# Early keys, values and q loaded with four rows to a partition, pooled keys out transposed, q turned by products with the identity

## The chip, the cores and the metric

The kernel runs on one core of one Trainium2 chip. The metric is the device time of one execution in microseconds (us), as the median of several runs. Lower is better.

## What is computed

Three stages in a row, all in float32: attention of every token over keys and values that are averaged in groups of 8 rows, an expert with a squared ReLU, and a gated expert.

```python
batch, n_heads, seq, head_dim = (8, 8, 576, 64)
k_p = k.reshape(B, H, Sp, pool, D).mean(axis=3)        # pool = 8, Sp = 72
v_p = v.reshape(B, H, Sp, pool, D).mean(axis=3)
scores = scale * np.matmul(q, k_p.transpose(0, 1, 3, 2))
attn = np.exp(scores - np.max(scores, axis=-1, keepdims=True))
attn = attn / (np.sum(attn, axis=-1, keepdims=True) + 1e-09)
x = np.matmul(attn, v_p)                               # then (B * S, H * D) = (4608, 512)
x = np.maximum(x @ w_in, 0.0) ** 2 @ w_out             # d_ff = 2048
out = (1.0 / (1.0 + np.exp(-(x @ w_gate))) * (x @ w_val)) @ w_out2   # d_ff = 1536
```

The weights of both experts arrive as 64-bit floats and are rounded to 32 bits on the chip.

## The kernel before

The 4608 tokens are worked in nine blocks of 512. The first expert runs block by block in passes over its 16 column tiles f: for each f four groups of three products make h (line 798), ScalarE and VectorE square it and split it into a high and a low part (lines 841 to 854), and twelve products with the output weights add to four banks (line 807). A float32 product is made of three products of such high and low parts. The first pass takes block 0 and only the tiles f = 0 to 7, the second takes block 1 and all 16.

Each weight tile has to be converted before its first use: a load of 512 KB (`raw_w`), a 64-bit add on GpSimd (line 235), one step on ScalarE (line 241), four on VectorE (lines 245 to 256), a copy of the high part on ScalarE (line 272) and a subtraction on VectorE (line 276). 32 such conversions (`in` 0 to 15, `out` 0 to 15) run during the first two passes.

Ahead of the first pass stands the attention of block 0, and within it that of block 1. Their keys, values and q come in by `early_kv` and `early_q`, which this change touches; the attention of later blocks is prepared in another way (`prep`, `load_q`) and is untouched. Before, an early k or v is loaded as three tiles with two rows of each head to a partition. Pooling is then a product with the constant `pm` as the stationary operand, 72 columns wide, and 512 columns of data moving (`pool_rows`, line 641). Pooled keys are copied to SBUF (line 674), turned by four transposes (line 679) and placed in `kpT` by two copies (line 683). q is loaded as it lies, one row to a partition, and is turned by 16 transposes of 128x128 (line 722). After that come scores (line 456), softmax in pieces on VectorE and ScalarE (lines 478 to 511), a turn of the weights (line 534), a copy (line 542), and the product with v (line 553).

The order of all instructions on each engine is written out beforehand by a planner (`Plan.run`). It simulates the engines with given durations (`op("pe", 0.88, ...)`), ranks and buffers, and each engine then runs its list strictly in that order. Loads and stores all stand in the list of SyncE (SP). The loaded tiles of early k, v and q lie in slots of the weight tiles; `convert_w1(n)` puts its raw tile in the slot of weight n + 4, so it waits until a load that was there has been used up. The numbers `n1 - 8` and so on in the calls choose these slots.

Of the kernel before, what the change touches and what calls it, by code (L numbers as in the profile page):

```python
# [131 lines left out]
def kernel(  # L132
# [12 lines left out]
    nc = tc.nc  # L145
# [197 lines left out]
    pm = att.tile([128, 160], F32, name="pm")  # L343
# [284 lines left out]
    rows = [(0, 128), (128, 128), (256, S // 2 - 256)]  # L628

    def load2(src, be, j, get):  # L630
        t = get()
        r0, rn = rows[j]
        nc.sync.dma_start(
            out=t[0:rn], in_=src[be, :, 2 * r0:2 * (r0 + rn), :].rearrange("h (p r) d -> p h (r d)", r=2))
        return t

    def pool_rows(src, st, j, r, bank):
        if j == 0 and r == 0:
            st["p"] = ps(*bank)
        r0, rn = rows[j]  # L640
        nc.tensor.matmul(
            out=st["p"][0:SP, :], lhsT=pm[0:rn, 64 - r0 // 4:64 - r0 // 4 + SP], rhs=src[j][0:rn, :, r],
            start=(j == 0 and r == 0), stop=(j == 2 and r == 1))

    def early_kv(be, src, n, rank, bank, consts, is_k):
        tiles, st = {}, {}
        prev, lds = [], []
        hold = be > 0
        for j in range(3):
            def ld(j=j):  # L650
                tiles[j] = load2(src, be, j, lambda: wpool.tile(
                    [128, H, 2, D], F32, tag=w1_tag(n + j), name="rows2"))

            lds.append(op("dma", (2.0, 2.0, 0.6)[j], ld, rank=rank + 0.1 * j, take=(w1_tag(n + j),), lag=2.0))
        for j in range(3):
            for r in range(2):
                o = op("pe", 0.88, lambda j=j, r=r: pool_rows(tiles, st, j, r, bank),
                       (lds if hold else lds[j:j + 1]) + prev + consts, rank + 4,
                       take=(bank[0],) if j == 0 and r == 0 else (), give=(w1_tag(n + j),) if r else ())
                prev = [o]  # L660
# [4 lines left out]

        if not is_k:
            o = op("act", 0.5, evac_v, prev, rank + 6, give=(bank[0],))
            for h in range(H):
                v_ready[be, h] = o
            return  # L670

        def evac_k():
            st["kp"] = kp = att.tile([SP, DM], F32, tag="kv", name="kp0", bufs=3)
            nc.scalar.activation(out=kp, in_=st["p"][0:SP, :], func=ACTF.Copy)

        def tr():
            st["p"] = p = ps(*bank)
# [10 lines left out]
        o = op("act", 0.5, evac_k, prev, rank + 5, take=("kv",), give=(bank[0],))  # L688
        o = op("pe", 0.3, tr, [o], rank + 6, take=(bank[0],), give=("kv",))
        o = op("act", 0.3, lambda: place(0), [o], rank + 7)  # L690
        o = op("act", 0.3, lambda: place(1), [o], rank + 7, give=(bank[0],))
# [3 lines left out]
    def early_q(b, rank, later, gets, takes, out_of, out_take, banks, consts):  # L695
        tiles = {}
        loads = []
        for hf in range(2):
            for j in range(NTA):
                def ld(j=j, hf=hf):  # L700
                    if j % 2 == 0 and hf == 0:
                        tiles["s"] = gets[j // 2]()
                    if hf == 0:
                        tiles[j] = tiles["s"][:, j % 2]
# [702 lines left out]
```

## Time and profile before

| What | Value |
|---|---|
| median of 3 runs | 1755.55 us (1755.24 to 1757.31) |
| profiled execution, its own time | 1755.72 us |
| its span | 1753.9 us |
| TensorE (PE) busy | 1732.8 us, 99% |
| VectorE (DVE) busy | 1103.3 us, 63% |
| ScalarE (ACT) busy | 799.3 us, 46% |
| GpSimd (POOL) busy | 239.5 us, 14% |
| mean granted TensorE clock | 0.993 of full speed |

The time is the span and 1.8 us around it. Busy means that an engine has an instruction under way. The shares are means over the whole execution: the change concerns its first 70 us or so, and has to be read from there.

### The profile page before, as it was taken

What the parts mean: (1) busy time and instruction counts of PE and PEld (TensorE: products, weight loads), DVE (VectorE), ACT (ScalarE), POOL (GpSimd) and SP (SyncE); (2) the same over time, 40 slices, a digit from 0 to 9 for tenths busy, and PEclk for the clock granted to TensorE, in tenths of its full rate; (3) what the DMA queues carried; (4) which work ended last, traced back from release to release, by engine and by line L of the source; (5) the groups of instructions that cost most, each with busy time, mean ns of one, the idle gap of its engine ahead of it and who ended that gap; (6) DMA issues with size and microseconds to landing.
All of it is one profiled execution on the core that took longest, in us unless ns stands there. A gap on an engine that the chain in (4) does not pass through costs nothing.

```text
span 1753.9 us, 24006 instructions
## 1 busy us (share of the span) xinstructions
PE 1732.8 (99%) x8624; PEld 1491.5 (85%) x8624; DVE 1103.3 (63%) x2066; ACT 799.3 (46%) x1946; POOL 239.5 (14%) x186
## 2 busy tenths in 40 slices
PE   7999999999999999999999999999999999999999
PEld 4678877878888888878888999999999999999998
DVE  7999758888686765523465555555555665655554
ACT  5676654453444343322345444445444444444442
POOL 1600000010001000000131112122111212111100
PEclk9999999999999999999999999999999999999999
DMA  9732244554544333020111222223333333333321
GB/s 259 267 88 74 53 104 106 148 155 121 142 106 128 99 95 105 31 86 1 60 49 61 72 73 85 73 97 120 109 109 109 120 120 120 109 109 109 108 73 49
DMA packets 183063, 179.71 MB, mean 102 GB/s; under 512 B 79008, under 2 KB 124832, under 8 KB 182944
## 3 DMA queue, kind: packets, MB, share of 16 engines
q1 hardware_dynamic: 182944, 178.18, 34.1%
q8 instruction: 68, 1.11, 0.3%
q14 instruction: 51, 0.42, 0.1%
HBM read 120.59 MB, written 49.28 MB: 97 GB/s over the span
## 4 chain that ended last, share of the span: by engine, by line
PE 93%; DMA 0%; DVE 0%; ACT 0%; issue 0%; ACTq 0%
PE acc L807 21%; PE h L798 21%; PE h L1190 17%; PE acc L1305 17%; PE att L1190 9%; PE acc L1190 4%; PE att L553 2%; PE att L456 2%; DMA y_dram<-y 0%; PE att L399 0%; ACT x L789 0%; DVE kp L390 0%; DVE e L511 0%; DVE g L854 0%; DVE o L1331 0%
## 5 line engine op out<-in xcount | busy, mean ns | idle before, releaser
L807 PE MATMUL acc<-g,out 128*128 128x512 f32 x1728 | 422.0, 393 | 0.0
L798 PE MATMUL h<-x,in 128*128 128x512 f32 x1728 | 421.0, 392 | 0.0
L807 PEld LDWEIGHTS acc<-g,out 128*128 128x128 f32 x1728 | 320.9, 188 | 72.7 <-issue 4.7
L798 PEld LDWEIGHTS h<-x,in 128*128 128x128 f32 x1728 | 321.3, 188 | 69.7 <-issue 2.0
L841 ACT ACTIVATE r<-h 128x512 f32<-128x512 f32 x144 | 86.0, 597 | 281.7 <-PE h L798 269.7
L1305 PE MATMUL acc<-in,p 128*128 128x512 f32 x648 | 182.6, 390 | 0.0
L1305 PE MATMUL acc<-out,p 128*128 128x512 f32 x648 | 182.2, 389 | 0.0
L847 DVE TENSOR_TENSOR r<-r,h 128x512 f32<-128x512 f32 x112 | 76.5, 684 | 133.7 <-ACT r L841 133.5
L1212 ACT ACTIVATE res<-h 128x384 f32<-128x384 f32 x144 | 70.7, 492 | 193.3 <-PE h L1190 187.0
L1305 PEld LDWEIGHTS acc<-out,p 128*128 128x128 f32 x648 | 121.6, 188 | 25.8
L1305 PEld LDWEIGHTS acc<-in,p 128*128 128x128 f32 x648 | 121.3, 188 | 23.9
L854 DVE TENSOR_TENSOR g<-r,g 128x512 fp32r<-128x512 f32 x144 | 103.4, 718 | 47.8 <-ACT g L851 46.4
L235 POOL INT64_ADD raw<-raw x40 | 43.7, 1093 | 592.1 <-DMA raw<-in_moe_w_out_dram 285.9
L851 ACT ACTIVATE g<-r 128x512 fp32r<-128x512 f32 x144 | 91.1, 633 | 67.9 <-DVE r L847 63.2
L1221 DVE TENSOR_TENSOR res<-res,acc 128x384 f32<-128x384 f32 x72 | 39.6, 551 | 120.4 <-PE acc L1190 116.8
L1331 DVE TENSOR_TENSOR o<-o,acc 128x512 f32<-128x512 f32 x72 | 49.4, 688 | 93.9 <-PE acc L1305 93.8
L1190 PE MATMUL h<-in,in 128*128 128x384 f32 x432 | 99.8, 339 | 3.8 <-ACT res L1212 3.8
L486 ACT ACTIVATE e<-att,m 128x72 f32<-128x72 f32 x272 | 82.9, 320 | 38.3 <-DVE m L478 38.2
L1190 PE MATMUL h<-out,in 128*128 128x384 f32 x432 | 99.7, 338 | 0.0
L1023 POOL TENSOR_TENSOR yt<-yf 128x768 f32<-128x768 f32 x32 | 59.8, 1870 | 291.9 <-DMA yf<-y_dram 257.4
L1271 ACT ACTIVATE p<-res 128x384 fp32r<-128x384 f32 x144 | 73.7, 523 | 55.7 <-DVE res L1265 55.5
L1190 PE MATMUL h<-in,out 128*128 128x384 f32 x432 | 98.0, 334 | 0.0
(140 smaller groups left out, 2707.0 us busy)
## 6 DMA issues: line engine op xcount, KB each, us to landing
yf<-y_dram SPq DMA_DIRECT2D x16, 1536.0 KB
o_part<-o SPq DMA_DIRECT2D x72, 256.0 KB
o<-o_part SPq DMA_DIRECT2D x72, 256.0 KB
y_dram<-y SPq DMA_DIRECT2D x36, 256.0 KB
w_dram<-t SPq DMA_DIRECT2D x36, 256.0 KB
w2s<-w_dram SPq DMA_DIRECT2D x36, 256.0 KB
out_dram<-o SPq DMA_DIRECT2D x36, 256.0 KB
raw_w<-in_moe_w_in_dram SPq DMA_DIRECT2D x15, 512.0 KB
```

The costliest lines, as they stand in the source:

```text
L486: nc.scalar.activation(out=e[:, h, 0:SP], in_=p[:, h * SP:(h + 1) * SP], func=ACTF.Exp, bias=m[:, h:h + 1], accum_out=z[:, h:h + 1])
L798: nc.tensor.matmul(out=h[:, 0:n], lhsT=w[:, a, kk * 128:(kk + 1) * 128], rhs=xs[kk][:, c], start=(kk == 0 and i == 0), stop=(kk == KT - 1 ...
L807: nc.tensor.matmul(out=y_ps[m][:, 0:NA], lhsT=w[:, a, m * 128:(m + 1) * 128], rhs=g_t[f][:, c], start=(f == f0 and i == 0), stop=(f == f1 ...
L841: nc.scalar.activation(out=r, in_=st["h"][:, 0:NA], func=ACTF.Relu)
L847: nc.vector.tensor_tensor(out=st["r"], in0=st["r"], in1=st["h"][:, 0:NA], op=ALU.mult)
L851: nc.scalar.activation(out=g[:, 0], in_=st["r"], func=ACTF.Copy)
L854: nc.vector.tensor_tensor(out=g_t[f][:, 1], in0=st["r"], in1=g_t[f][:, 0].bitcast(F32), op=ALU.subtract)
L1023: nc.gpsimd.tensor_tensor(out=t, in0=q(a), in1=q(c), op=ALU.subtract)
L1190: nc.tensor.matmul(out=st[which, z][:, 0:HN], lhsT=w[:, wa, col:col + 128], rhs=ys[y, k2][:, yc], start=(first[z] == m and k2 == 0 and j = ...
L1212: nc.scalar.activation(out=new((which, key)), in_=st[which, z][:, 0:HN], func=ACTF.Copy)
L1271: nc.scalar.activation(out=p_t[fi][:, 0, h * HN:(h + 1) * HN], in_=st["gate", key], func=ACTF.Copy)
L1305: nc.tensor.matmul(out=o_ps[i], lhsT=p_t[f][:, a, i * 128:(i + 1) * 128], rhs=wslot[c, "out", f][:, w], start=(f == 0 and j == 0), stop=(f ...
```

## The change

Early k and v are now loaded as four tiles, two for each half of the heads, with four rows of each head to a partition: 128 partitions (64 pooled rows' worth) and 16 partitions (8 pooled rows' worth). `pm` is 64 columns wide and sums two partitions. For k the data is now the stationary operand, 64 columns (one head) at a time, and `pm` moves with 64 or 8 columns; heads 2i and 2i + 1 go to the lower and the upper 64 partitions of the result, which is thus already turned. The copy to SBUF and the four transposes fall away. For v `pm` stays stationary, with 64 and 8 columns, and 256 columns of data move. q comes as one tile for each half of the heads with four rows to a partition, and is turned by full products with the identity, 64 columns stationary and 128 moving, which write every fourth column. The planner gets new durations, and the loads take other slots.

```diff
-        nc.vector.memset(pm, 0.0)
-            out=pm[:, 64:96], in_=ident.rearrange("p (n r) -> p n r", r=POOL // 2), op=ALU.add, axis=AX.X)
+            out=pm, in_=ident.rearrange("p (n r) -> p n r", r=POOL // 4), op=ALU.add, axis=AX.X)
-    rows = [(0, 128), (128, 128), (256, S // 2 - 256)]
-    def pool_rows(src, st, j, r, bank):
-        nc.tensor.matmul(
-            out=st["p"][0:SP, :], lhsT=pm[0:rn, 64 - r0 // 4:64 - r0 // 4 + SP], rhs=src[j][0:rn, :, r],
-            start=(j == 0 and r == 0), stop=(j == 2 and r == 1))
+    R = 4
+    rows = [(0, 128), (128, S // R - 128)]
+    def pool_values(src, st, bank):
+        for hf in range(2):
+            for r in range(R):
+                n0 = 0
+                for j, (_, rn) in enumerate(rows):
+                    n = rn * R // POOL
+                    nc.tensor.matmul(
+                        out=st["p"][n0:n0 + n, 256 * hf:256 * hf + 256], lhsT=pm[0:rn, 0:n],
+                        rhs=src[hf, j][0:rn, :, r], start=(r == 0), stop=(r == R - 1), skip_group_check=True)
+                    n0 += n
+    def pool_keys_t(src, st, hf, bank):
+        for pr in range(2):
+            n0 = (2 * hf + pr) * SP
+            for j, (_, rn) in enumerate(rows):
+                n = rn * R // POOL
+                for r in range(R):
+                    for i in range(2):
+                        nc.tensor.matmul(
+                            out=st["p"][64 * i:64 * i + 64, n0:n0 + n], lhsT=src[hf, j][0:rn, 2 * pr + i, r],
+                            rhs=pm[0:rn, 0:n], start=(r == 0), stop=(r == R - 1), skip_group_check=True)
+                n0 += n
...
-        def evac_k():
-        def tr():
-            for pr in range(KT):
-                nc.tensor.transpose(
-                    p[:, pr * SP:(pr + 1) * SP], st["kp"][:, pr * 128:(pr + 1) * 128], ident[0:SP, 0:SP])
...
-                for j in range(NTA):
-                    nc.tensor.transpose(
-                        p[:, 128 * j:128 * (j + 1)], tiles[j][:, 2 * pr:2 * pr + 2].rearrange("p h d -> p (h d)"), ident)
+                for r in range(R):
+                    for i in range(2):
+                        nc.tensor.matmul(
+                            out=p[64 * i:64 * i + 64, r:NA:R], lhsT=tiles[hf][:, 2 * (pr % 2) + i, r], rhs=ident,
+                            start=True, stop=True)
...
-    early_kv(0, k, n1 - 8, -0.5, ("acc3", 1), [c2], True)
+    early_kv(0, k, n1 - 20, -0.5, ("acc3", 1), [c2], True)
-    early_kv(0, v, n1 - 14, V0L, ("acc3", 1), [c2], False)
+    early_kv(0, v, n1 - 16, V0L, ("acc3", 1), [c2], False)
-    early_kv(1, k, n1 - 17, t1 - P1, K1B, [c2], True)
+    early_kv(1, k, n1 - 12, t1 - P1, K1B, [c2], True)
-    early_kv(1, v, n1 - 11, t1 - P1 + V1L, K1B, [c2], False)
+    early_kv(1, v, n1 - 8, t1 - P1 + V1L, K1B, [c2], False)
```

The planner's order moves with it. In the rows below the tile names carry a number for the buffer; `rows` are the loaded tiles, `kp` pooled keys, `att`, `h` and `acc` PSUM banks.

First place: TensorE's list from its start to the first scores. Before (key pooling, turns of pooled keys, first half of q, scores):

```order
L641 MATMUL acc_102<-rows_95,pm 72x512 x2
L641 MATMUL acc_102<-rows_98,pm 72x512 x2
L641 MATMUL acc_102<-rows_100,pm 72x512 x2
L679 MATMUL acc_126<-ident,kp_122 128x72 x4
L722 MATMUL acc_146<-ident,rows_112 128x128 x2
L722 MATMUL acc_146<-ident,rows_119 128x128 x2
L456 MATMUL att<-kpT_78,qT_158 128x144 x2
L456 MATMUL h<-kpT_78,qT_158 128x144 x2
```

After, of the same place:

```order
L654 MATMUL acc_105<-pm,rows_94 64x64 x8
L654 MATMUL acc_105<-pm,rows_97 64x8 x8
L726 MATMUL acc_189<-ident,rows_q 64x128 x8
L726 MATMUL acc_200<-ident,rows_q 64x128 x8
L726 MATMUL acc_218<-ident,rows_q 64x128 x8
L726 MATMUL acc_230<-ident,rows_q 64x128 x8
L455 MATMUL att<-kpT_78,qT_209 128x144 x2
L455 MATMUL h<-kpT_78,qT_209 128x144 x2
```

All of q's turns now stand ahead of the first scores, where only the first half of them stood.

Second place: ScalarE's list from the first exponentials on (`e` softmax weights, `vp` pooled values, `aT` turned weights). Before:

```order
L486 ACTIVATE e,z<-att,m 128x72 x4
L499 ACTIVATE e<-e 128x4x72
L486 ACTIVATE e,z<-att,m 128x72 x4
L499 ACTIVATE e<-e 128x4x72
L664 ACTIVATE vp<-acc_193 72x512
L726 ACTIVATE qT_250<-acc_238 128x512
```

After:

```order
L485 ACTIVATE e,z<-att,m 128x72 x4
L498 ACTIVATE e<-e 128x4x72
L485 ACTIVATE e,z<-att,m 128x72 x4
L677 ACTIVATE vp<-acc_276 72x512
L541 ACTIVATE aT<-acc_319 72x16x32
L541 ACTIVATE aT<-acc_333 72x16x32
L498 ACTIVATE e<-e 128x4x72
```

The fourth exponential of the first half now stands behind the copy of pooled values and behind two copies of turned weights.

Third place: TensorE's list at the end of the first pass, where the last turns of block 1's attention weights stand (line 534 before, 533 after). Before:

```order
L798 MATMUL h<-x,in_142 128x512 x6
L399 MATMUL att<-ident,kp 128x72
L534 MATMUL att<-ident,e_80 72x128 x4
L399 MATMUL att<-ident,kp 128x72
L534 MATMUL att<-ident,e_81 72x128 x4
L807 MATMUL acc_612<-g,out_1114 128x512 x3
L807 MATMUL acc_618<-g,out_1114 128x512 x3
```

After:

```order
L803 MATMUL h<-x,in_216 128x512 x6
L812 MATMUL acc_767<-g,out_1189 128x512 x3
L812 MATMUL acc_777<-g,out_1189 128x512 x3
L812 MATMUL acc_788<-g,out_1189 128x512 x3
L812 MATMUL acc_795<-g,out_1189 128x512 x3
L398 MATMUL att<-ident,kp 128x72
L533 MATMUL att<-ident,e_80 72x128 x4
L533 MATMUL att<-ident,e_81 72x128 x4
```

The last twelve products of the pass now stand ahead of the two turns, and stood behind them.

## Rows read from the trace of the kernel before

**Rows 1.** The page, its first lines: busy us (share of span) xinstructions.

```profile
span 1753.9 us, 24006 instructions
...
PE 1732.8 (99%) x8624; PEld 1491.5 (85%) x8624; DVE 1103.3 (63%) x2066; ACT 799.3 (46%) x1946; POOL 239.5 (14%) x186
```

**Rows 2.** Windows by stage: busy us of each engine, TensorE's clock, DMA share, GB/s.

```profile
16.00:35.00 19.00, 18.06 (x78) 11.02 (x79) 16.59 (x38) 13.34 (x50) 4.29 (x4) 0.85 1.17 291
35.00:54.70 19.70, 19.14 (x52) 6.37 (x50) 19.43 (x31) 10.81 (x20) 11.09 (x9) 0.74 0.97 319
54.70:77.00 22.30, 19.86 (x105) 15.86 (x105) 21.09 (x28) 17.79 (x43) 16.46 (x13) 1.00 0.97 331
77.00:111.00 34.00, 34.00 (x186) 27.02 (x185) 29.44 (x63) 26.12 (x78) 1.15 (x1) 1.00 0.08 20
111.00:115.00 4.00, 2.02 (x15) 1.49 (x14) 3.86 (x12) 2.63 (x12) 0.00 (x0) 1.00 0.36 69
115.00:930.00 815.00, 815.00 (x3887) 662.26 (x3886) 547.50 (x1042) 359.24 (x970) 65.13 (x60) 1.00 0.35 94
```

**Rows 3.** Waits of TensorE over the span: us in total, times, longest.

```profile
PE acc L641 <- DMA rows<-in_k_dram: 5.0, 1, 5.0
PE att L534 <- DVE e L511: 4.4, 4, 1.3
PE att L456 <- ACT qT L726: 2.1, 1, 2.1
```

**Rows 4.** Timeline of TensorE, 0 to 55 us: start, us, what [idle before].

```profile
5.01 6.95 PE L641 MATMUL acc<-rows,pm 128*72 128x512 f32 x12 [5.01 <-DMA rows<-in_k_dram]
12.74 0.44 PE L679 MATMUL acc<-ident,kp 72*128 72x72 f32 x4 [0.78 <-ACT kp L674]
13.02 1.04 PE L722 MATMUL acc<-ident,rows 128*128 128x128 f32 x8
...
31.48 1.08 PE L553 MATMUL acc<-aT,vp 72*64 72x512 f32 x4
32.49 0.76 PE L456 MATMUL h<-kpT,qT 128*128 128x144 f32 x4
...
34.19 2.79 PE L641 MATMUL att<-rows,pm 128*72 128x512 f32 x6
36.82 1.47 PE L534 MATMUL acc<-ident,e 128*72 128x128 f32 x12
...
54.66 1.66 PE L798 MATMUL h<-x,in 128*128 128x512 f32 x6
```

**Rows 5.** Timeline of TensorE, a product with v in block 1.

```profile
91.80 1.10 PE L553 MATMUL att<-aT,vp 72*64 72x64 f32 x12
92.83 3.02 PE L798 MATMUL h<-x,in 128*128 128x512 f32 x12
```

**Rows 6.** Timeline of SyncE's queue, the early loads of q and what follows.

```profile
4.33 6.63 SPq L708 DMA_DIRECT2D rows<-in_q_dram  x6
...
29.91 7.87 SPq L708 DMA_DIRECT2D rows<-in_q_dram  x10
37.82 0.50 SPq L231 DMA_DIRECT2D raw_w<-in_moe_w_out_dram  x1
```

**Rows 7.** Windows of 2 us, columns as in rows 2.

```profile
18.00:20.00 2.00, 2.00 (x11) 2.00 (x10) 1.92 (x5) 1.77 (x10) 0.00 (x0) 0.50 1.14 243
...
46.00:48.00 2.00, 2.00 (x7) 0.38 (x4) 2.00 (x3) 1.25 (x3) 2.00 (x2) 0.50 1.05 391
```

**Rows 8.** Groups of VectorE: line 251 in 42.5 to 77.3, then 77.3 to 124.

```profile
L251 DVE SCALAR_TENSOR_TENSOR t_w<-raw_w,t_w 128x512 uint32<-128x512 uint32 x5 | 6.4, 1283 | 0.2
...
L251 DVE SCALAR_TENSOR_TENSOR t_w<-raw_w,t_w 128x512 uint32<-128x512 uint32 x9 | 6.2, 684 | 0.0
```

**Rows 9.** Timeline of GpSimd's adds, and of VectorE at TensorE's second wait.

```profile
45.96 10.11 POOL L235 INT64_ADD raw_w<-raw_w  x7 [0.32 <-DMA raw_w<-in_moe_w_out_dram]
...
73.73 0.96 DVE L511 TENSOR_TENSOR e<-e,z 128x288 f32<-128x288 f32 x1
```

More of the change, by code (lines that the diff above doesn't have):

```diff
@@ L645, in early_kv @@
     def early_kv(be, src, n, rank, bank, consts, is_k):
         tiles, st = {}, {}
[L647 to L660, printed above, removed]
+        lds = []
@@ new lines, in early_kv, with ld @@
+        for hf in range(2):
+            for j, (r0, rn) in enumerate(rows):
+                x = 2 * hf + j
+                def ld(hf=hf, j=j, r0=r0, rn=rn, x=x):
+                    tiles[hf, j] = t = wpool.tile([128, 4, R, D], F32, tag=w1_tag(n + x), name="rows4")
+                    nc.sync.dma_start(
+                        out=t[0:rn],
+                        in_=src[be, 4 * hf:4 * hf + 4, R * r0:R * (r0 + rn), :].rearrange("h (p r) d -> p h (r d)", r=R))
+                lds.append(op("dma", (1.65, 0.3)[j], ld, rank=rank + 0.1 * x, take=(w1_tag(n + x),), lag=2.0,
+                              after=lds[-1:]))
@@ L664, in evac_v @@
             nc.scalar.activation(out=vp_t[be].rearrange("n h d -> n (h d)"), in_=st["p"][0:SP, :], func=ACTF.Copy)
+        tags = tuple(w1_tag(n + x) for x in range(4))
         if not is_k:
-            o = op("act", 0.5, evac_v, prev, rank + 6, give=(bank[0],))
+            o = op("pe", 3.5, lambda: pool_values(tiles, st, bank), lds + consts, rank + 4, take=(bank[0],), give=tags)
+            o = op("act", 0.6, evac_v, [o], rank + 6, give=(bank[0],))
             for h in range(H):
@@ L686, in place @@
                 scale=kscale)
[L688 to L691, printed above, removed]
+        prev = []
+        for hf in range(2):
+            o = op("pe", 1.8, lambda hf=hf: pool_keys_t(tiles, st, hf, bank),
+                   (lds if be else lds[2 * hf:2 * hf + 2]) + prev + consts,
+                   rank + 4, take=(bank[0],) if hf == 0 else (), give=tags[2 * hf:2 * hf + 2])
+            prev = [o]
+        o = op("act", 0.4, lambda: place(0), [o], rank + 7)
+        o = op("act", 0.4, lambda: place(1), [o], rank + 7, give=(bank[0],))
         for pr in range(KT):
@@ L698, in early_q, with ld @@
         for hf in range(2):
[L699 to L713 removed]
+            def ld(hf=hf):
+                tiles[hf] = t = gets[hf]()
+                for off, m, be, s0 in parts(b):
+                    nc.sync.dma_start(
+                        out=t[off // R:(off + m) // R],
+                        in_=q[be, 4 * hf:4 * hf + 4, s0:s0 + m, :].rearrange("h (p r) d -> p h (r d)", r=R))
+            loads.append(op("dma", 1.65, ld, rank=rank + later * hf, take=(takes[hf],), lag=2.0, after=loads[-1:]))
         res = []
@@ L727, in ev @@
                     out=out_of(pr).rearrange("p a g t -> p (a g t)"), in_=st["p"], func=ACTF.Copy)
[L729 to L731 removed]
+            o = op("pe", 0.9, tr, [loads[hf]] + consts, rank + 5 + pr, take=(bank[0],),
+                   give=(takes[hf],) if pr % 2 else ())
+            res.append(op("act", 0.6, ev, [o], rank + 6 + pr, take=(out_take(pr),) if out_take(pr) else (),
                           give=(bank[0],)))
```

33 lines of the change are left out of this document (7 added, 26 removed).

## The prediction

> **What bounds the kernel now.** I start with the page. TensorE is busy for 1732.8 of 1753.9 us [rows 1], so only 21 us are there to be won by waiting less, and the rest by giving TensorE less to do. The windows by stage say where: from 115 to 930 us TensorE never pauses [rows 2]. An early gain is therefore kept in full, and an early loss is paid in full: what counts is when TensorE gets to the end of the first pass, at about 115 us. The list of its waits gives 5.0 us for the first keys, 2.1 us for turned q and 4.4 us in four pieces for softmax weights from VectorE [rows 3]. There is no wait for any other early load in it.
>
> Next I put TensorE and VectorE side by side, stage by stage [rows 2]. From 16 to 35 us TensorE is idle for 0.94 us and VectorE for 2.41; from 35 to 54.7 us it is 0.56 and 0.27; from 54.7 to 77 us 2.44 and 1.21. So after 16 us two engines are full at once. VectorE's work there is softmax and the conversion of weights, and this change takes none of it away. It is also slow there: one step of a conversion (line 251) takes 1283 ns up to 77 us and 684 ns behind that [rows 8], and the difference goes with GpSimd, which adds without pause from 46 to 56 us [rows 9] and for 16.46 us of the window to 77 [rows 2]. From 77 to 111 us TensorE alone is full. From 111 to 115 us it waits again for VectorE, 1.98 us. So there are two places where TensorE is tied to VectorE: about 73 to 75 us, where VectorE's last step before the second turn starts at 73.73 [rows 9], and 111 to 115 us. A gain on TensorE ahead of 73 us is only worth what VectorE brings along.
>
> **The change part by part.** All prices of TensorE are for its higher clock (2.4 GHz) first.
>
> Pooling before: three products take 2.63 us, from 34.19 to 36.82 [rows 4], 0.877 us each. There are 24 (two keys, two values, six each): 21.0 us. Turning pooled keys: 0.44 us [rows 4] twice, 0.9. Turning q: 8 transposes in 1.04 us [rows 4], 16 for each block: 4.2 us for both. Sum 26.1 us.
>
> After, everything but the scores is 64 columns wide, with two results in different halves of the partitions. The trace has such products in line 553: 64 wide, in pairs. One pair with 512 columns takes 1.01 us, from 31.48 to 32.49 [rows 4], where two products of that length one after another would take 1.75. So a pair does lie side by side. In block 1 two pairs with 64 columns and one with 384 take 1.03 us, from 91.80 to 92.83 [rows 5]; the long one is 0.75 x 1.01 = 0.76, which leaves 0.135 us for a short pair.
> - One k: 16 pairs with 64 columns moving and 16 with 8. At 0.135 us each 4.3 us. No row shows 8 columns moving; from below they cost 8/512 of 1.01 us, 0.016, and the 64-column pairs 0.126, together 2.3 us. I take 4.3, since the short pair is the nearest row and is itself dearer than its columns.
> - One v: eight times 256 columns for 64 rows, with the 8-row product in the upper half beside it: 8 x 0.505 = 4.0 us. If these two don't lie side by side it is 16 x 0.44 = 7.0 us.
> - One q: 16 pairs with 128 columns, 0.25 us each, 4.0 us; singly 7.0.
>
> After in all 2 x (4.3 + 4.0 + 4.0) = 24.6 us, so TensorE's work shrinks by 1.5 us, with bounds of 5.5 us less (k at 2.3) and, with nothing side by side (k then 8.6), 19 us more. The gain in work is small: the products are shorter but there are many more.
>
> Here a rule speaks against the change. The Trainium skill, TensorEngine Tiling (Array Packing), section Key Properties, says that a change of tiling mode drains TensorE, and v's products change between 128 partitions by 64 columns and 16 partitions by 8 at every step. By the rule v would be nearer to 7.0 than to 4.0. No row here changes mode at every product, so this stays among the rivals.
>
> ScalarE loses two copies of pooled keys. It is not full in any of these stages [rows 2], so I set them at nothing. VectorE loses one clear and sums twice as many columns of the constant, both ahead of 5.0 us, where everything waits for keys: nothing.
>
> Loads: the same bytes. For q six issues took 6.63 us of SP's queue, and ten took 7.87 us [rows 6]; now it is two and four. The first raw tile behind all early loads is issued at 37.82 [rows 6]; it will go out several microseconds sooner. What it triggers is that GpSimd's adds start sooner, and so does VectorE's slow phase, partly over softmax. I price this at nothing: as many adds fall on as much work, only earlier.
>
> Order: all of q's turns stand ahead of the first scores, an extra 2.0 us at the high clock. They have to wait for the second half of q, but ScalarE's copies hold the scores back anyway (2.1 us before [rows 3]). If that cover is gone, first scores come 1 to 2 us later. On ScalarE the fourth exponential now stands behind the copy of pooled v and two copies of turned weights. Queued behind it are the exponentials of the second half, and VectorE waits for these. Both go against the gain.
>
> The likeliest sum. VectorE's idle time from 16 to 77 us is 2.41 + 0.27 + 1.21 = 3.9 us, and it is idle because TensorE and ScalarE are late with scores and exponentials. With pooling of v shorter I let it win back three quarters: -2.9 us, with bounds from +3 (the two new waits above) to -3.9. At the second tie the last twelve products of the pass, 3.0 us of work [rows 5], now stand ahead of the two turns and fill the 1.98 us [rows 2]; but they wait for VectorE's last conversion, so I count two thirds: -1.3 us, with bounds 0 and -2. Everything between is filled with the same work as before. 1755.7 - 2.9 - 1.3 = 1751.5 us. It is made against the profiled execution (1755.72, a span of 1753.9 and 1.8 around it), which is 0.2 us above the median.
>
> **The rivals.**
> 1. The loads bound the start. For: DMA's share is 1.17 and 0.97 through the first stages [rows 2], with only 243 GB/s at 18 to 20 us, among the early loads in pieces of 256 and 512 bytes, and 391 GB/s at 46 to 48 us, among raw weights [rows 7]. The Trainium skill, DMA: Bandwidth & Descriptors, section Specifications, asks for 512 bytes or more for full rate. By that rule, the trace agrees in direction. Against: no wait of TensorE names an early load after the first [rows 3]. If it were so: four loads of 1.18 MB, two of 1.05 and six raw tiles of 0.52 are 10 MB by 37.8 us, some 280 GB/s; at 331 [rows 2] to 391 GB/s [rows 7] they would be there 6 to 10 us sooner, and the end would move by 8: 1748 us.
> 2. The gain is eaten. VectorE waits as much as before behind ScalarE's new order, and the conversions come no sooner: 1755.5 us. For: both engines are full, and TensorE's work hardly shrinks.
> 3. The clock, on the other side. TensorE ran at 0.50 of its clock, its 1.2 GHz level, around 18 to 20 us, where it had waited, and again around 46 to 48 us, busy throughout with line 553 and pooling [rows 7], and stood at 0.74 in the mean of 35 to 54.7 us [rows 2]. Short products with few partitions and pauses for loads could give more of that. 10 us more at the low level cost TensorE 5 us and come in place of the gain: 1760 us. It decides from the point where TensorE has no more idle time ahead of 73 us, about 3 to 4 us of extra work.
> 4. v's products don't lie side by side, because they change between 128 and 16 partitions at every step: 3.0 us more for each v, 6.0 in all, less the 1.5 saved: 4.5 us more on an engine that has some 4 us of idle time to 77 us; with the second tie relieved by the 1.3 us some 1759 us. This is what the Trainium skill's rule on tiling modes, named above, would make of it.
>
> **How the numbers follow.** Chances: forecast 0.38, rival 1 0.20, rival 2 0.21, rival 3 0.14, rival 4 0.07. The predicted time is 1751.5. The forecast's own range is 1750 to 1755.5 (the two terms between their lower bounds and nothing). What a measurement can tell here is about 0.2%, 3.5 us, so faster means under 1752.1. Of the forecast two thirds lie there, 0.25, with all of rival 1: 0.45. The other third with rival 2 is the same: 0.34. Rivals 3 and 4 are slower: 0.21. The range for 8 in 10 takes in rival 1 down to 1744 and most of rivals 3 and 4: 1744 to 1760.
>
> **What would show it.** Right: k pooling at about 4.3 us and v at 4.0 at the high clock; first product of the first expert well ahead of 54.66 [rows 4]; VectorE under 1 us idle in each stage to 77 us; no wait of TensorE at the end of the first pass; unbroken TensorE from there to the next stage change. Wrong: VectorE idle for several microseconds between 16 and 45 us with ScalarE named (rival 2); clock 0.50 over more than the 16 us that the means 0.85 and 0.74 make in 16 to 54.7 us [rows 2] (3); v near 7 us (4); or the end of the first pass 6 us or more earlier, with VectorE keeping pace because conversions begin sooner (1). The prediction is also wrong if the planner's shifted order costs or frees something after 115 us, which I set at nothing.

## The result, and the profile after

The change makes the kernel slower: 1765.6 us median (1764.6 to 1767.59, 4 runs) against 1755.5 for the kernel before, a ratio of 1.0056 with a 95% interval of 1.0043 to 1.0068. Forecast was 1751.5 us. The profiled execution has a span of 1762.8 us, 8.9 more than before [rows 1]. One of the twelve executions of e19 below took twice as long (3494.8 us) and isn't in its ratio.

First lines of the page of the changed kernel, columns as in [rows 1]:

```profile
span 1762.8 us, 24719 instructions
...
PE 1742.1 (99%) x8984; PEld 1504.3 (85%) x8984; DVE 1102.5 (63%) x2065; ACT 800.5 (45%) x1944; POOL 241.5 (14%) x186
```

TensorE is busy for 9.3 us more, and waits for as long as before: 20.7 us in all, 21.1 before. So the loss is work of TensorE, or the same work at the lower clock. How far it has grown by the end of the first expert is told by the windows from the start to TensorE's wait at the change to the gated expert, of before and then of after:

```profile
0.00:930.56 930.56, 916.89 (x4340) 727.32 (x4340) 644.30 (x1222) 434.92 (x1177) 100.85 (x94) 0.99 0.39 108
```

```profile
0.00:939.39 939.39, 925.96 (x4700) 739.95 (x4700) 643.68 (x1221) 436.56 (x1175) 103.12 (x94) 1.00 0.39 107
```

All of the 8.8 us is there by then. Groups of TensorE's instructions over these stretches (busy us, mean ns of one | idle before) say which work it is. Before, pooling and turning q:

```profile
L641 PE MATMUL att<-rows,pm 128*72 128x512 f32 (+1 forms) x24 | 14.4, 736 | 0.0
L641 PE MATMUL acc<-rows,pm 128*72 128x512 f32 (+1 forms) x24 | 13.1, 694 | 5.0 <-DMA rows<-in_k_dram 5.0
L722 PE MATMUL att<-ident,rows 128*128 128x128 f32 x16 | 2.2, 272 | 0.0
L722 PE MATMUL acc<-ident,rows 128*128 128x128 f32 x16 | 2.1, 276 | 0.0
```

Turning pooled keys, with the shapes kept apart:

```profile
L679 PE MATMUL att<-ident,kp 72*128 72x72 f32 x4 | 0.7, 324 | 0.0
L679 PE MATMUL acc<-ident,kp 72*128 72x72 f32 x4 | 0.4, 233 | 0.8 <-ACT kp L674 0.8
```

After, values (L639), keys (L654) and q (L726), and the second product of the experts (L812):

```profile
L812 PE MATMUL acc<-g,out 128*128 128x512 f32 x1728 | 424.4, 394 | 3.7 <-DVE g L859 3.7
...
L639 PE MATMUL acc<-rows,pm 128*64 128x256 f32 (+1 forms) x32 | 8.9, 390 | 0.0
L639 PE MATMUL att<-rows,pm 128*64 128x256 f32 (+1 forms) x32 | 8.9, 390 | 0.0
L654 PE MATMUL acc<-pm,rows 128*64 128x64 f32 (+1 forms) x128 | 8.1, 286 | 5.4 <-DMA rows<-in_k_dram 5.4
L726 PE MATMUL acc<-ident,rows_q 128*64 128x128 f32 x64 | 5.5, 352 | 0.0
L654 PE MATMUL att<-pm,rows 128*64 128x64 f32 (+1 forms) x128 | 4.8, 213 | 0.0
L726 PE MATMUL att<-ident,rows_q 128*64 128x128 f32 x64 | 4.2, 277 | 0.0
```

Before, pooling took 27.5 us, turning keys 1.1 and q 4.3, 32.9 in all. After, it is 17.8 for values, 12.9 for keys and 9.7 for q, 40.4 in all: 7.5 us more, where the prediction had 1.5 us less. These are sums at mixed clocks. With everything at the high clock it was 26.1 us before, by the prediction's prices, and is about 35.7 by the rows below (twice 8.87, 4.8 and 4.2): 9.6 us more, nearly all of it for values. The clock hides some of that: from 16 to 54.7 us it stood at 0.85 and 0.74 before [rows 2] and at 1.00 after, which is worth some 8 us of TensorE's work, an estimate from these means. The first expert's products take 3.5 us more (846.5 against 843.0), and other lines somewhat less.

The windows by stage answer to [rows 2]:

```profile
16.00:35.00 19.00, 17.88 (x124) 10.56 (x120) 14.16 (x34) 9.59 (x37) 4.56 (x4) 1.00 1.10 291
35.00:54.70 19.70, 19.16 (x203) 10.07 (x203) 17.54 (x28) 11.93 (x29) 11.67 (x10) 1.00 0.90 306
54.70:77.00 22.30, 18.64 (x118) 13.34 (x118) 20.96 (x26) 15.63 (x39) 13.21 (x12) 0.96 0.89 308
77.00:111.00 34.00, 33.86 (x175) 25.69 (x173) 31.46 (x68) 25.13 (x68) 2.60 (x2) 0.93 0.05 13
111.00:115.00 4.00, 4.00 (x23) 3.45 (x22) 3.11 (x6) 3.76 (x8) 0.00 (x0) 1.00 0.08 9
115.00:130.00 15.00, 13.22 (x74) 9.13 (x73) 13.77 (x26) 11.41 (x35) 0.00 (x0) 1.00 0.43 127
```

VectorE, which was to win back its idle time, loses more of it: 4.84 us idle from 16 to 35 us (2.41 before) and 2.16 from 35 to 54.7 (0.27 before). The wait at 111 to 115 us is gone, as foreseen, but 1.78 us of waiting come behind it, at 115 to 130. The rate of the loads hardly changed, 291 GB/s from 16 to 35 us in both.

The timeline of TensorE answers to [rows 4]:

```profile
5.40 8.10 PE L654 MATMUL acc<-pm,rows 128*64 128x64 f32 x128 [5.40 <-DMA rows<-in_k_dram]
13.43 5.49 PE L726 MATMUL acc<-ident,rows_q 128*64 128x128 f32 x64
18.84 0.76 PE L455 MATMUL att<-kpT,qT 128*128 128x144 f32 x4
...
21.00 8.87 PE L639 MATMUL acc<-rows,pm 128*64 128x256 f32 x32
...
37.31 2.38 PE L654 MATMUL att<-pm,rows 128*64 128x64 f32 x64
...
40.18 2.43 PE L654 MATMUL att<-pm,rows 128*64 128x64 f32 x64
...
53.92 0.96 PE L803 MATMUL h<-x,in 128*128 128x512 f32 x3
...
75.80 5.06 PE L812 MATMUL acc<-g,out 128*128 128x512 f32 x11 [3.66 <-DVE g L859]
```

Each pooled value takes 8.87 us at the high clock. The second keys take 2.38 + 2.43 us at the high clock, but the first take 8.10, which is what they take at the low one: the profile's clock has no entry so early, but in e4 below one half of the second keys takes 4.03 us at a granted clock of 0.50, and in e14 the first keys take 4.78. Behind the wait of 3.66 us at 72 to 75.8 the clock is at 0.50 for some 7 us (eleven products of the expert take 5.06 us, 0.46 each instead of 0.24).

While TensorE pools the first value, VectorE has nothing to do: its timeline shows a wait of 3.72 us, and later the steps L245 that begin the third and the fourth conversion of weights.

```profile
30.96 0.46 DVE L477 TENSOR_REDUCE m<-att 128x4 f32<-128x288 f32 x1 [3.72 <-PE att L455]
...
42.52 1.26 DVE L245 TENSOR_SCALAR t_w<-t_w 128x512 f32<-128x512 f32 x1
46.47 1.25 DVE L245 TENSOR_SCALAR t_w<-t_w 128x512 f32<-128x512 f32 x1
```

In the kernel before, these two steps stood here:

```profile
28.67 0.43 DVE L245 TENSOR_SCALAR t_w<-t_w 128x512 f32<-128x512 f32 x1 [0.41 <-ACT t_w L241]
29.48 0.42 DVE L245 TENSOR_SCALAR t_w<-t_w 128x512 f32<-128x512 f32 x1
```

They come 14 and 17 us later, and take 1.25 us each instead of 0.42. The reason for the delay isn't data. GpSimd's adds for these weights were over by 26 us, but ScalarE, whose step L241 goes ahead of L245, takes up the third only at 41.11 (GpSimd, then ScalarE):

```profile
24.43 1.31 POOL L235 INT64_ADD raw_w<-raw_w  x1 [0.32 <-DMA raw_w<-in_moe_w_in_dram]
40.81 1.04 POOL L235 INT64_ADD raw_w<-raw_w  x1 [15.08 <-DMA raw_w<-in_moe_w_out_dram]
```

```profile
41.11 0.70 ACT L241 ACTIVATE t_w<-raw_w 128x512 f32<-128x512 f32 x1
```

By then GpSimd is at its next adds, and VectorE's steps are the slow ones of [rows 8].

### The profile page after: what moved, and what is told of

Read it like the earlier page. It is cut to its first block, busy times and chain, and to the rows that moved or that the text cites. A ratio compares the mean times of both kernels' runs of the same rounds, so it can differ in the third digit from the quotient of the medians.

```text
span 1762.8 us, 24719 instructions
## 1 busy us (share of the span) xinstructions
PE 1742.1 (99%) x8984; PEld 1504.3 (85%) x8984; DVE 1102.5 (63%) x2065; ACT 800.5 (45%) x1944; POOL 241.5 (14%) x186
## 4 chain that ended last, share of the span: by engine, by line
PE 94%; DVE 0%; DMA 0%; ACT 0%; issue 0%; ACTq 0%
PE acc L812 22%; PE h L803 22%; PE h L1195 17%; PE acc L1310 17%; PE att L1195 9%; PE acc L1195 4%; PE att L455 2%; PE att L552 2%; DMA y_dram<-y 0%; PE att L533 0%; PE att L398 0%; DVE e L510 0%; DVE vp L389 0%; DVE kp L389 0%; DVE t_w L251 0%
## 5 line engine op out<-in xcount | busy, mean ns | idle before, releaser
L812 PE MATMUL acc<-g,out 128*128 128x512 f32 x1728 | 424.4, 394 | 3.7 <-DVE g L859 3.7
L812 PEld LDWEIGHTS acc<-g,out 128*128 128x128 f32 x1728 | 322.4, 189 | 76.2 <-issue 4.6
```

The source lines that it names most:

```text
L812: nc.tensor.matmul(out=y_ps[m][:, 0:NA], lhsT=w[:, a, m * 128:(m + 1) * 128], rhs=g_t[f][:, c], start=(f == f0 and i == 0), stop=(f == f1 ...
```

## The experiments

Five theories go through the expectations. T1: values cost TensorE too much, since their products change shape at every step. T2: the start, that is keys at the low clock and all of q's turns ahead of the scores. T3: the planner's order of the other engines' work. T4: the losses overlap on two engines that are both full. T5: keys by themselves. T6, formed later, is T3 at one place, ScalarE's queue. "Before" was measured beside each run, at 1755.5 to 1756.1 us. A ratio to it stands in each row. Two rows that differ by under some 2 us are not told apart by their intervals. "Equal" stands for values padded to equal shapes, explained below.

| run | keys, values, q | else | us | ratio (95%) |
|---|---|---|---|---|
| after | new, new, new | | 1765.6 | 1.0056 (1.0043 to 1.0068) |
| e1_v_grouped | new, new, new | v by shape | 1764.9 | 1.0057 (1.0044 to 1.0071) |
| e2_v_old | new, old, new | | 1762.6 | 1.0045 (1.0033 to 1.0057) |
| e3_q_old | new, new, old | | 1762.7 | 1.0043 (1.0031 to 1.0055) |
| e4_warm | new, new, new | 6 products added | 1776.3 | 1.0108 (1.0081 to 1.0136) |
| e5_k_old | old, new, new | | 1767.2 | 1.0063 (1.0049 to 1.0077) |
| e6_k_alone | new, old, old | | 1757.1 | 1.0009 (1.0000 to 1.0018) |
| e7_v_alone | old, new, old | | 1767.1 | 1.0064 (1.0052 to 1.0077) |
| e8_q_alone | old, old, new | | 1764.2 | 1.0047 (1.0034 to 1.0059) |
| e9_v_pad | new, equal, new | | 1763.1 | 1.0042 (1.0030 to 1.0055) |
| e10_v_pad_alone | old, equal, old | | 1754.3 | 0.9994 (0.9985 to 1.0003) |
| e11_k_v_pad | new, equal, old | | 1757.9 | 1.0012 (1.0003 to 1.0022) |
| e12_v_planned | new, new, new | v planned 8.9 us | 1765.6 | 1.0059 (1.0046 to 1.0072) |
| e13_k_planned | new, new, new | k planned 4.0 us | 1761.0 | 1.0030 (1.0018 to 1.0043) |
| e14_pad_warm3 | new, equal, new | 3 products added | 1762.6 | 1.0038 (1.0025 to 1.0051) |
| e15_pad_k_planned | new, equal, new | k planned 4.0 us | 1756.9 | 1.0009 (1.0001 to 1.0018) |
| e16_pad_k_q | new, equal, new | the same, half of q later | 1756.7 | 1.0006 (0.9996 to 1.0016) |
| e18_q_alone_hold | old, old, new | half of q later | 1765.5 | 1.0056 (1.0042 to 1.0069) |
| e19_k_v_planned | new, equal, old | k planned 4.0 us | 1757.7 | 0.9999 (0.9989 to 1.0009) |

**Values in another order, and each part undone.** In e1 the loops of values are turned round:

```diff
-        for hf in range(2):
-            for r in range(R):
-                for j, (_, rn) in enumerate(rows):
+        for j, (_, rn) in enumerate(rows):
+            for hf in range(2):
+                for r in range(R):
+                    n0 = 64 * j
```

e2 and e3 put back the functions of the kernel before for one part, with their loads, in the slots of the change. e4 adds products whose result nobody reads:

```diff
+    def warm():
+        p = ps("h", 2)
+        for i in range(6):
+            nc.tensor.matmul(out=p, lhsT=ident, rhs=..., start=True, stop=True)
```

> The changed kernel with one thing different: in the pooling of values all eight products with 128 rows come first and then the eight with 16, so TensorE goes from the one tile shape to the other once instead of at every product. Same products, same plan. T1 (the alternation is what makes pooled v 8.87 us instead of 4.0): each v falls to 16 x 0.213 to 0.44 us, that is 3.4 to 7.0 us, the row's steps become even (0.213 to 0.22 us each), and the time falls by 2 to 5 us, to about 1761 to 1763. T2 (the loss comes from the start: keys at the low clock and q turned in 5.5 us ahead of the scores): v may get shorter, the first scores stay at 18.8 us and the time stays within 1.5 us of 1765.6. T3 (order on ScalarE): as T2.

> The changed kernel with values loaded and pooled as before (three loads with two rows to a partition, six products of 512 columns, 5.3 us at the high clock); keys and q as changed. T1 (the new pooling of v, 3.6 us longer each and in one piece ahead of the second half's scores, is the main loss): VectorE's wait of 3.7 us at 31 us and TensorE's of 3.7 us at 75 us go, and the time falls by 6 to 9 us to about 1757 to 1760. T2 (start): it stays above 1762. T3: 1763 to 1766.

> The changed kernel with q loaded and turned as before (six loads in rows, 16 transposes for each block, turned in two halves); keys and values as changed. T2 (q's products, all ahead of the scores, delay the start): first scores come 1 to 2.6 us sooner, at 16.2 to 17.8 us, VectorE's first conversion too, and the time falls by 3 to 5 us to about 1761 to 1763. T1: v stays at 8.87 us, the time stays within 2 us of 1765.6. If the loads in short pieces of before are themselves a loss, it rises.

> The changed kernel with six added products of the identity with 512 zeroed columns ahead of the first keys, in the wait for them (up to 5.4 us); their result is not used. T2 (the low clock up to 17.1 us is a large part of the loss): the granted clock rises ahead of or within the first keys, keys take 4.8 to 6 us instead of 8.03, q 4.2 to 5 instead of 5.4, the first scores come at 14.5 to 17 us, and the time falls by 2 to 4 us. T1: the start gets shorter, but VectorE still waits behind pooled v, and the time falls by under 1.5 us. If the products end only behind the keys' arrival, the first keys start later than 5.4 us and part of the gain is lost.

The row of values in e1, in the timeline of TensorE:

```profile
22.07 7.21 PE L639 MATMUL acc<-rows,pm 128*64 128x256 f32 x32
```

7.21 us instead of 8.87, with 14 changes of shape fewer: 0.12 us for each. But 7.21 us for 16 products is 0.45 each, the price of products one after another. So the alternation is the smaller part, and grouping can't bring the rest, since products of one shape then write the same half. The time didn't move. e2 and e3 each took about 3 us off (2 by the ratios, with intervals that overlap that of the change), the least that T2 said for q and half or less of what T1 said for values. In e2 TensorE was busy for 7.4 us less than after and waited 5.4 us more (1734.7 and 26.1 us of its span): T4. e4 came out far slower: keys did shrink to 4.78 us, but their start slipped to 9.27, and from 37 to 70 us TensorE was busy throughout at a granted clock of 0.50, with the same keys, values and q. Half of the second keys in it:

```profile
38.94 4.03 PE L654 MATMUL att<-pm,rows 128*64 128x64 f32 x64
```

Its times go from 1765.9 to 1782.2, and the profile is of the slowest; whether the others had the low stretch too is not shown.

**One part alone.** These complete the eight combinations of three parts.

> The changed kernel with keys loaded, pooled and turned as before; values and q as changed. T1 (pooled values) and T2 (q's products): the loss stays, 1763 to 1767. T5 (keys: 128 short products at the low clock hold everything else back by 2 to 3 us, and leave the clock low for q): first scores come sooner than 18.8 us, and the time falls by 3 to 5 us to 1761 to 1763. What the two runs before showed goes in here: values as before brought 3.0 us and q as before 2.9 us, so no single part can hold the whole 10 us, and T4 says that the parts' losses overlap on two engines that are both full.

> The kernel before with the change made for keys alone; values and q as before. T1 and T2: within 2 us of before, 1754 to 1757.5. T5 (keys are a loss by themselves): 1758 to 1761. T3 (a planner's order that any change of costs upsets is worth several us by itself): over 1758 too, but with TensorE's time in keys no longer than before.

> The kernel before with the change made for values alone. T1: the row's 8.87 us for each value stays, and the time is 1760 to 1765 (twice 3.6 us more work at the high clock, on an engine with some 4 us of idle time). T2, T5: under 1758. T4 (losses overlap): 1758 to 1762.

> The kernel before with the change made for q alone, which takes six loads in 256-byte pieces away and turns q by 64 products. T2: first scores 1 to 2 us later than 16.2 us, 1758 to 1762. T1, T5: within 2 us of before, 1754 to 1757.5. Rival 1 of the prediction (loads bound the start): faster, 1748 to 1752.

All "alone" runs keep the slots that the change gave to the loads, so none shows the slots by themselves; e6 bounds them together with keys. T5 falls: keys alone cost some 1.6 us, at the edge of noise, and putting them back in the change gained nothing. Values alone cost 11.3 us, q alone 8.3, both together (e5) 11.4: the losses overlap, T4. In e7 the second value in the timeline of TensorE, where the first takes 8.87 us:

```profile
43.98 16.02 PE L643 MATMUL att<-rows,pm 128*64 128x256 f32 x32
```

It runs at the low level, 0.50 in the window from 44 to 66 us, which began soon behind a wait of 0.80 us; TensorE was busy all the time and the clock did not come back before 67. In the kernel before, the mean of 0.74 over 19.7 us makes about 10 us of low clock at this place [rows 2]. So part of e7's 11.3 us is clock, and not the values' work. q alone was no faster than before, so larger pieces of its loads gave no gain that shows (rival 1 of the prediction).

**Values with equal shapes, and values planned at their length.** e9 clears the second tile of values ahead of its load and sends all of its 128 partitions through the product, e10 does so for values alone and e11 with new keys beside them, and e12 changes a number of the planner:

```diff
-                        out=st["p"][n0:n0 + n, 256 * hf:256 * hf + 256], lhsT=pm[0:rn, 0:n],
-                        rhs=src[hf, j][0:rn, :, r], ...
+                        out=st["p"][64 * j:64 * j + 64, 256 * hf:256 * hf + 256], lhsT=pm,
+                        rhs=src[hf, j][:, :, r], ...
```

```diff
-            o = op("pe", 3.5, lambda: pool_values(tiles, st, bank), ...
+            o = op("pe", 8.9, lambda: pool_values(tiles, st, bank), ...
```

> The changed kernel with one thing different: the second tile of values is cleared by VectorE ahead of its load (four clears of about 1 us in VectorE's idle time before 11 us), and all 128 of its partitions go through the product with all 64 columns of the pooling matrix, so that both products of a pair have one shape (128 rows by 64 columns) and write the two halves of the partitions. Same number of products, same plan otherwise. T1a (v's products don't lie side by side because their shapes differ): v falls from 8.87 to about 4.0 us, the prediction's own price, TensorE's work by some 9.7 us; the time then tells what the rest of the change is worth, 1751 to 1757 if the prediction's other terms hold, 1757 to 1761 if q's products and the start cost what the run with q alone showed. T1b (two results of one accumulation bank are written one after another whatever the shapes): v stays at 7 to 9 us and the time at 1763 to 1766.

> The kernel before with values alone changed, in the form with equal shapes. T1a: each v takes about 4.0 us (5.3 before), and the time falls from 1767 with the first form to 1752 to 1756. T1b: 1765 to 1768.

> The kernel before with keys changed as in the change and values in the form with equal shapes; q as before. T1a: by the runs so far keys alone were within 2 us of before, and q alone cost 8 us; without q's part the time is 1751 to 1757, below the run with all three parts. If keys delay the start by more than values bring back, 1757 to 1760.

> The changed kernel with one number different: the planner is told 8.9 us for pooling of values instead of 3.5, so it orders all engines' work by the duration that the trace shows. T3 (a good part of the loss is an order made for too short an operation): the waits of VectorE (3.7 us at 31 us) and TensorE (3.7 us at 75 us) shrink, and the time falls by 2 to 5 us to 1761 to 1763. T1 (the work itself is too long): within 2 us of 1765.6.

In e9 the timeline of TensorE has

```profile
21.02 3.67 PE L638 MATMUL acc<-rows,pm 128*64 128x256 f32 x32
39.73 3.67 PE L638 MATMUL att<-rows,pm 128*64 128x256 f32 x32
44.91 0.96 PE L810 MATMUL h<-x,in 128*128 128x512 f32 x3
...
55.85 1.22 PE L810 MATMUL h<-x,in 128*128 128x512 f32 x2 [4.12 <-DVE x L804]
```

3.67 us, with the same count of products into the same bank: T1a holds and T1b falls. Values alone then go from 1767.1 to 1754.3 us: 10.4 us less work, and less time at the low clock (mean 0.92 from 54.7 to 77 us in e10, 0.71 in e7). With all three parts TensorE reaches the first expert at 44.91, 9.0 us sooner than after, and is soon stopped: 4.12 us of waiting for VectorE, and 21.3 us of waits up to the end of the first expert where after had 13.4. So 2.5 us are left of 10.4 us less work, hardly more than the intervals. e12 shifted waits about (6.2 us for ScalarE's copies at 52 to 59 us, with the conversions at 28.7) and gained nothing.

**What holds VectorE back.** e15 and e13 tell the planner how long the first keys take, e16 and e18 also hold the second half of the first q behind the four scores of its first half (in e18 too, whose expectation speaks of two), and e14 has three added products instead of six, which start earlier:

```diff
-            o = op("pe", 1.8, lambda hf=hf: pool_keys_t(tiles, st, hf, bank),
+            o = op("pe", 1.8 if be else 4.0, lambda hf=hf: pool_keys_t(tiles, st, hf, bank),
```

```diff
+    for pr in range(2, KT):
+        score_ops[0, 0, 3]["next"].append(turn_ops[0, pr])
+        turn_ops[0, pr]["left"] += 1
```

> The run with all three parts and equal shapes, with one number different: the planner is told 4.0 us instead of 1.8 for each half of the first keys, which is what they take. ScalarE's two first conversion steps then stand ahead of its copies of pooled keys, not behind them. T6 (ScalarE in its order holds VectorE back until pooled keys are there): VectorE's first conversion step comes at 11 to 12 us instead of 15.1, TensorE's wait of 4.1 us for VectorE at 55 us goes, and the time falls from 1763 to 1757 to 1760. T2 (q's turns ahead of the scores) and the clock: within 1.5 us of 1763.

> The run before, and the second half of the first q is turned only behind the first four scores, as in the kernel before. T2 (the second half's turns delay the first scores and with them VectorE): first scores 1 to 2 us sooner, 1754 to 1757. If T6 alone holds the loss: as the run before it. If neither: 1762 or more, and the loss is in the work of q's products themselves.

> The kernel before with q alone changed, and the second half of the first q turned only behind the first two scores. T2: first scores at 17.5 to 18.5 us instead of 19.8, and the time falls from 1764 to 1757 to 1760. If the loss of q is elsewhere (its low-clock work, copies in four pieces, the second q's turns): 1762 to 1765.

> The run with all three parts and equal shapes, with three added products of the identity with 512 zeroed columns in the wait for the first keys. Clock theory (keys and q at the low clock until 17.1 us cost the start 3 to 4 us): the first keys start up to 1 us later but take 4.8 to 6 us instead of 8.1, the first scores come at 16 to 17 us instead of 18.9, VectorE's first conversion at 12 to 13 us instead of 15.1, and the time falls to 1758 to 1761. If the start isn't what holds the loss: within 1.5 us of 1763.

> The changed kernel with one number different: the planner is told 4.0 us instead of 1.8 for each half of the first keys. Values stay in the form with unequal shapes, 8.87 us each. ScalarE's steps for the second two weight conversions move ahead of the second half's softmax, so VectorE makes them at about 28 us, ahead of GpSimd's adds (from 40 us), not at 42.5 us among them. If order and shapes are two losses that add up: the time falls by some 6 us to 1758 to 1761. If either alone keeps the loss (with equal shapes alone it fell by 2.5 us, and both together by 8.7): 1762 to 1764. If the order doesn't count while values are long: 1765 to 1767.

> The kernel before with keys changed, values in the form with equal shapes, q as before, and the planner told 4.0 us for each half of the first keys. The run without that number was 1757.9, with the second conversions at 29.9 us already. If ScalarE's copy of pooled keys ahead of the first conversions (VectorE's start at 15.1 us) still costs there: 1753 to 1756, level with before or a little under it. If not: 1757 to 1759.

One number of the planner took 6.2 us off e9, and 4.6 off the change as it is. In the changed kernel ScalarE's next L241 behind the first two is the one at 41.11 shown above, behind the exponentials of the second half and both copies of x. In e13 the next two stand ahead of them, around the copy of pooled values (L677):

```profile
22.15 0.67 ACT L241 ACTIVATE t_w<-raw_w 128x512 f32<-128x512 f32 x1
29.21 0.59 ACT L677 ACTIVATE vp<-acc 72x512 f32<-72x512 f32 x1 [6.39 <-PE acc L639]
29.71 0.66 ACT L241 ACTIVATE t_w<-raw_w 128x512 f32<-128x512 f32 x1
```

VectorE's steps L245 of the third and fourth conversion, from the timelines of e13 and then of e15:

```profile
33.12 0.42 DVE L245 TENSOR_SCALAR t_w<-t_w 128x512 f32<-128x512 f32 x1
39.13 0.42 DVE L245 TENSOR_SCALAR t_w<-t_w 128x512 f32<-128x512 f32 x1
```

```profile
28.10 0.42 DVE L245 TENSOR_SCALAR t_w<-t_w 128x512 f32<-128x512 f32 x1
34.10 0.42 DVE L245 TENSOR_SCALAR t_w<-t_w 128x512 f32<-128x512 f32 x1
```

They are ahead of the next adds again, at 0.42 us each. In e9, from which e15 differs by the number alone, they came at 38.71 and 41.66, and it was the steps behind them that took 1.25 to 1.52 us among the adds. VectorE has done 58.90 us of work from 12 to 77 us in e15, against 56.77 in e9, 53.51 after and 60.77 before. In e13 it is only 54.97; there TensorE is busy for 4.0 us less than after (1738.1) and waits as long (20.6): its wait of 3.66 us has shrunk to 1.08, and the low clock behind it is gone.

That the first two conversions are not what counts is told by e14. There the keys fell to 4.78 us and the first conversion came at 12.98 us instead of 15.10, but the third only at 37.9; the time stayed at 1762.6. So T6 as it was put (VectorE's start) is not borne out, and shorter first keys are worth less than 1.5 us there. That the third and fourth are what counts is argued and not shown. The number moves other rows too: in e13 and e15 only two of the first four scores stand ahead of pooled values on TensorE. And an early third conversion (21.5 to 29.5 us) isn't enough: e12 (values at 8.87 us, and the wait named above), e3, e8 and e18 have it at 1762.7 to 1765.6 us. Nor does VectorE's work up to 77 us set the order by itself: e18 has done 63.39 us of it, and e6 only 55.01 at 1757.1. e16 is level with e15: where the second half of q is turned doesn't matter there.

e19 and e10 are the versions that could have beaten the kernel before. Both are level with it.

## Why the prediction was wrong

- **One v at "8 x 0.505 = 4.0 us".** This step failed, and it is the larger in TensorE's work: 8.87 us each, 9.7 us more for the two. The price came from a pair of equal shapes (line 553, [rows 4]) and was put on a pair of unequal ones. With equal shapes it is right, 3.67 measured. The upper bound of 7.0 was the serial price, and e1 shows 7.21; the rest is the alternation. Rival 4 had the mechanism, and a price of 3.0 for each v that was too low by 1.9.
- The Trainium skill, TensorEngine Tiling (Array Packing), section Key Properties, says that a change of mode drains TensorE. The trace agrees: some 0.12 us for a change. The larger loss here is that the two don't run beside each other at all.
- **"Everything between is filled with the same work as before", and "Order".** The second step that failed. The paragraph on order listed what moved on ScalarE around the exponentials, but not that the third and fourth conversion moved behind them, from 28.67 to 42.5 us. That could have been read from the order of the rows, without a run. "As many adds fall on as much work, only earlier" is wrong for the same reason: conversions that lay in GpSimd's pause (from 26.7 to 42.6 us before) now lie in its adds. The planner's number, which mends this, brings 4.6 us as the change stands, and 6.2 with equal shapes, so in time this step is the larger. That these rows are what makes its gain is argued.
- The two steps add up to nearly all: 1765.6 us with neither mended, 1763.1 and 1761.0 with one, 1756.9 with both, against 1755.5. Equal shapes bring 2.5 us without the other and 4.1 with it, which fits two engines that are both full to 77 us, as the prediction said of gains; the difference of 1.6 us is within the noise.
- **VectorE's idle time, of which the prediction let it win back three quarters: -2.9 us.** It grew instead, from 3.9 us to 8.3 in the three windows from 16 to 77 us: 4.4 more, where the bound was +3. The wait of 3.72 us at 27 to 31 is most of that. Nothing of the gain came even with both steps mended: e15 is 1.0009 of before. In its profiled execution, which is level with that of before, TensorE does less (915.7 us up to the end of the first expert, 916.9 before), and waits 15.4 us instead of 13.7. That is rival 2.
- **The second tie, -1.3 us**: the 1.98 us did go, and came again as 1.78 us at 121 to 128.
- **Keys at 4.3 us and q at 4.0 us at the high clock**: right (4.8 for the second keys, 4.2 for the second q). But the first keys and part of the first q ran at the low clock, 8.10 and 5.49 us, which the prediction, pricing all at the high clock "first", never added. Before, the first keys took 6.95 us with products of 512 columns [rows 4]. By e14 this matters little for the end.
- **Rival 1** (loads bound the start): no. The rate stayed at 291 GB/s, no later load is waited for, and q alone with its larger pieces lost 8 us.
- **Rival 3** (clock): as a rival for the whole it is wrong, since the mean clock was higher than before in 16 to 54.7 us. Behind the wait of 3.66 us the low stretch to 82 us cost about 3 us, by the same products at either level (eleven of the expert 2.4, eight turns of weights 0.8).

What stays open: why q alone loses 8.3 us. Its turns take 6 us more than before there, and TensorE waits 4.9 us more to the end of the first expert. One wait is most of that: a row of the second q's turns stands ahead of the expert's products and waits 4.32 us for ScalarE's copy L802, which stands behind ScalarE's step L272, and this waits for a conversion that VectorE makes among the adds (TensorE, ScalarE, VectorE in e8):

```profile
63.20 1.98 PE L797 MATMUL att<-ident,rows_q 128*64 128x128 f32 x16 [4.32 <-ACT qT L802]
62.03 0.63 ACT L272 ACTIVATE in<-t_w 128x512 fp32r<-128x512 f32 x1 [3.24 <-DVE t_w L256]
60.48 1.52 DVE L256 SCALAR_TENSOR_TENSOR t_w<-raw_w,t_w 128x512 uint32<-128x512 uint32 x1
```

The clock is at 0.50 behind it, to some 69 us. A wait of about 4 us stands at such turns in e2 and e18 too (4.58 and 3.79, for ScalarE), and not before, after or in e15. That this wait and the clock behind it make the loss is argued; no run takes it away by itself. Holding half of the first q back (e18) didn't help, and together with new keys, equal shapes and the right number for the planner q costs 2 us at most (e15 against e19, 1.0009 and 0.9999, with intervals that meet). That turning q by transposes from the new layout would be cheaper wasn't tried either. And which of the rows that the planner's number moves makes the gain of e13 and e15 was not tried row by row.

## What to carry to other kernels

A price for a pair of products side by side holds for that pair of shapes alone: two of one shape lay side by side here, and two of different shapes did not. Padding the smaller one with cleared rows can be cheaper than leaving it small (3.67 us against 8.87). When a planner sets the order, compare the rows of every engine for the work that fills its pauses, not only around the change, and give it durations from a trace: here a duration of 1.8 us for what takes 4.0 put a conversion on another engine at 42.5 us, which comes at 33.1 with the right one. Two engines that are both full hide each other's losses and gains, so undo parts together as well as one by one.

## What the runs showed of the hardware that was not expected

- Products of 128 rows by 64 columns and of 16 rows by 8, with 256 columns moving, didn't overlap: 16 of them take 8.87 us alternating, and 3.67 when both have 128 rows and 64 columns (grouped by shape 7.21, where each group writes one half). Whether the rows or the columns must be equal wasn't tried.
- A TensorE that never paused stayed at its lower level for long. In e7 it was at 1.2 GHz (0.50) for 24 us, from soon behind a wait of 0.80 us, under pooled values (16.02 us for the row that takes 8.87) and what followed; in e4, behind waits of 0.98 and 0.68 us, for 34 us. The first keys took their low-clock time of 8.10 us throughout, and 4.78 in e14, where three products of 512 columns ran ahead of them:

```profile
1.59 5.06 PE L756 MATMUL h<-kpT,ident 128*128 128x512 f32 x6 [1.59 <-POOL ident masks.py:199]
6.59 4.78 PE L652 MATMUL acc<-pm,rows 128*64 128x64 f32 x128
```

- One step of VectorE with one input (L245) takes 0.42 us while GpSimd rests and 1.25 among its adds, three times as long. The Trainium skill, SBUF — State Buffer, section Who interferes with whom, says that such steps can share a port with GpSimd, and that the one that comes second waits for the other's whole instruction. The trace agrees in direction: the step takes 0.83 us longer, within the 1.04 of one add.
